# Two unused tiles in SBUF that shift what lies behind them, and the last first product one step earlier

## The chip, the cores and the metric

One core of a Trainium2 chip runs the kernel. The time is that of the device, in microseconds, for one launch; the kernel before was run three times. Beside these stands one profiled execution, of which the trace tells the start and duration of each instruction. In the views TensorE is PE (its weight loads PEld), VectorE is DVE, ScalarE is ACT, GpSimd is POOL, SyncE is SP.

## The reference

What is computed is a gated linear attention over 4 x 8 heads, 768 positions and head size 40, and behind it two feed-forward layers on 3072 tokens with 320 features and 2048 hidden units, all in float32:

```python
h = x @ w_in
g = np.maximum(h, 0.0) ** 2                                          # layer 0
g = np.where(h > 0.0, h, np.exp(np.minimum(h, 0.0)) - 1.0)           # layer 1
x = g @ w_out
```

The attention's output, heads side by side, is x of layer 0; the output of layer 0 is x of layer 1.

## The kernel before

**Tiles and steps.** The tokens are cut into 6 tiles of 512 (`NTILE`, `TT`), the hidden units into 16 blocks of 128 (`NF`). One step `k` is one layer, one token tile and one block of hidden units: 2 x 6 x 16 = 192 steps, 0 to 191, layer 0 first. Each float32 operand of a product is held as two fp32r parts, a high and a low one, and a product is the sum high x high + high x low + low x high.

- `mm1(k)`, the first product (L496): eight matmuls of 512 columns. A block of `w` is the stationary side, the tile's `xh` or `xl` the moving side; the sum is the PSUM tile `h`.
- `elem(k)` and `elem_lo(k)`, the elementwise part, into `ghi` and `glo`. In layer 0 ScalarE does most of it. In layer 1 ScalarE makes r, th and ex of h (L514, L515, L516), VectorE joins them (L517, L518, which reads h too), GpSimd rounds r into ghi (L519), and VectorE subtracts ghi from r into glo (L524).
- `mm2(k)`, the second product (L540). In layer 0 it is eight matmuls with `w` as the stationary and ghi or glo as the moving side, 512 columns. In layer 1 it is twelve, three for each of four accumulators, with ghi or glo as the stationary side and 320 columns of `w` as the moving one: ghi with the high weights, ghi with the low ones, glo with the high ones.
- `put(k)` at the last block of a tile copies the accumulators out and stores them.

**What sets the order.** The first 20 steps and much of the attention follow the table `ORDER`. From then on a loop over k writes the instructions: the first products up to step k + 2, their elementwise part, other work that is due, and then the second product of step k. So TensorE runs two first products ahead. On TensorE the order of the code is kept. In layer 1's last tile the other engines' instructions are placed by a scheduler when the kernel is built.

**Buffers.** Tiles are laid one behind the other in each SBUF partition, in the order of the pools: `const`, `w`, `raw`, `cvt`, `cvu`, `x`, `g`, `y`, and then the attention's. The `g` pool has two buffers each of `r`, `ghi` and `glo`, so those of step k are used again by step k + 2. The attention's pools are closed at layer 0's last tile, and the pools `by`, `bt`, `pa` and `pb` of layer 1 take their place. `h` has two buffers in `ph` and, from there on, two in `pb` for odd k.

Other matmuls that the prediction compares with: fillers without use (L659, bf16, 512 columns of ones, `dr`) and the three matmuls that make a mask early on (L613 to L615). L614's moving side `nst` is a row of 512 fp32r elements; L615's is `heads`, a view in which each value is repeated 128 times with step 0.

Of the kernel before, what the change touches and what calls it, by code (L numbers as in the profile page):

```python
# [6 lines left out]
F32 = mybir.dt.float32  # L7
F32R = mybir.dt.float32r
# [24 lines left out]
TT = 4 * L  # L33
# [30 lines left out]
def body(tc, qk, qp, kvo, gates, wq, ident_in, qkm_in, out):  # L64
# [4 lines left out]
    def pool(name, bufs=1, stack=es, **kw):  # L69
        return stack.enter_context(tc.tile_pool(name=name, bufs=bufs, **kw))  # L70
# [3 lines left out]
    negm_dr = dram.tile([NCH, B * H, L], F32, name="negm_dr")  # L74

    constp = pool("const")
    wp = pool("w", bufs=NF)
    rawp = pool("raw", bufs=3)
    cvt = pool("cvt", bufs=3)
    cvu = pool("cvu", bufs=2)  # L80
    xp = pool("x", bufs=2)
    gp = pool("g", bufs=2)
    yp = pool("y", bufs=3)
# [332 lines left out]
    def attn_pre(t):  # L416
        u, k = divmod(t, 4)
        if k == 0:
            units(u, lambda u: emit_E(2 * u))
            units(u - 1, norm)  # L420
            units(u + 1, kvo_load)
        elif k == 1:
            units(u, lambda u: emit_E(2 * u + 1), o_tanh, wk_mult)
            if u + 1 == NPLAIN // 2:
                qk_load(NPLAIN + 1)
        elif k == 2:
            units(u + 1, lambda v: qk_hi(2 * v), lambda v: qk_hi(2 * v + 1), lambda v: mask(2 * v))
            units(u + 1, lambda v: mask(2 * v + 1), lambda v: qk_stack(2 * v), lambda v: qk_stack(2 * v + 1))
        else:
            units(u + 2, lambda v: mb_load(2 * v), lambda v: mb_load(2 * v + 1), qp_load)  # L430
            units(u + 2, lambda v: qk_load(2 * v), lambda v: None if v == NPLAIN // 2 else qk_load(2 * v + 1))
        if k % 2 == 0:
            gate_at(t + 12, gate_store)
            if t == 10:
                gate_put(1)
            gate_at(t + 18, gate_load)

    def attn_pe(t):
        u, k = divmod(t, 4)
        if k == 0:  # L440
            units(u, lambda u: [f() for f in scores(2 * u)])
        elif k == 1:
            units(u - 1, lambda w: [f() for f in trans(w)])
            units(u, lambda u: [f() for f in scores(2 * u + 1)])
        for c in range(1, NCH):
            if t == (16 * c - 9 if c > 1 else 9):
                for f in gate_cols(c):
                    f()

    def attn_mul(t):  # L450
        u, k = divmod(t, 4)
        if k < 2:
            units(u, lambda u: emit_P(2 * u + k))
        if k == 1:
            units(u - 1, x_hi)
        if t % 16 == 7 and 0 < t // 16 < NCH - 1:
            gate_put(t // 16 + 1)

    def attn_post(t):
        u, k = divmod(t, 4)  # L460
        if k == 1:
            units(u - 1, x_lo)
        if k % 2:
            gate_at(t + 15, gate)
        else:
            gate_at(t + 14, gate_exp)
# [6 lines left out]
    def turn(t):  # L473
        for f in (attn_pre, attn_pe, attn_mul, attn_post, attn_last):
            f(t)

    G, HB, ACC = {}, {}, {}
    steps = [(l, j, m, (0, TT)) for l in range(2) for j in range(NTILE) for m in range(NF)]
    bp = {}

    def mm1(k):
        l, j, m, (c0, c1) = steps[k]
        n = c1 - c0
        w = W[l, m]
        xh, xl = X[l * NTILE + j]
        ilo = WC + (0 if l else 64)
        h = (bp["h"] if "h" in bp and k % 2 else ph).tile([128, TT], F32, tag="h", name="h")
        seq = []
        for kk in range(2):
            ws = slice(kk * 128, kk * 128 + 128)  # L490
            wlo = slice(ilo + kk * 128, ilo + kk * 128 + 128)
            seq += [(w[:, ws], xh[:, kk, c0:c1]), (w[:, ws], xl[:, kk, c0:c1]), (w[:, wlo], xh[:, kk, c0:c1])]
        seq += [(w[:, 256:384], xh[:, 2, c0:c1]), (w[:, ilo + 256:ilo + 384], xh[:, 2, c0:c1])]
        HB[k] = h
        return [
            lambda i=i, a=a, b_=b_: pe.matmul(h[:, 0:n], lhsT=a, rhs=b_, start=(i == 0), stop=(i == len(seq) - 1))  # L496
            for i, (a, b_) in enumerate(seq)
        ]

    def elem(k):  # L500
        l, j, _, (c0, c1) = steps[k]
        n = c1 - c0
        h = HB.pop(k)[:, 0:n]
        r = gp.tile([128, TT], F32, tag="r", name="r")[:, 0:n]
        hi = gp.tile([128, TT], F32R, tag="ghi", name="ghi")[:, 0:n]
        lo = gp.tile([128, TT], F32R, tag="glo", name="glo")[:, 0:n]
        if l == 0:
            act.activation(out=r, in_=h, func=AF.Relu)  # L508
            act.activation(out=hi, in_=r, func=AF.Square)  # L509
            act.activation(out=r, in_=r, func=AF.Square)  # L510
        else:
            th = bp["t"].tile([128, TT], F32, tag="th", name="th")
            ex = bp["t"].tile([128, TT], F32, tag="ex", name="ex")
            act.activation(out=r, in_=h, func=AF.Relu, scale=-1.0)  # L514
            act.activation(out=th, in_=r, func=AF.Tanh, scale=0.5)  # L515
            act.activation(out=ex, in_=r, func=AF.Exp, scale=-1.0)  # L516
            dve.scalar_tensor_tensor(out=ex, in0=ex, scalar=1.0, in1=th, op0=ALU.add, op1=ALU.mult)  # L517
            dve.scalar_tensor_tensor(out=r, in0=h, scalar=0.0, in1=ex, op0=ALU.max, op1=ALU.subtract)  # L518
            pool_.tensor_scalar(out=hi, in0=r, scalar1=1.0, scalar2=1.0, op0=ALU.mult, op1=ALU.mult)  # L519
        G[k] = (hi, lo, r)  # L520

    def elem_lo(k):
        hi, lo, r = G[k]
        dve.tensor_tensor(out=lo, in0=r, in1=hi.bitcast(F32), op=ALU.subtract)  # L524
# [213 lines left out]
    def first(k):  # L738
        nonlocal nm
        todo = []  # L740
        while nm <= min(k, len(steps) - 1):
            for f in mm1(nm):
                f()
            todo.append(nm)
            nm += 1
        return todo

    for k in range(NK, len(steps)):
        l, j, m, _ = steps[k]
        if k == (NTILE - 1) * NF:  # L750
            early.close()
            es.enter_context(tc.manual_schedule(engines={pe.engine}))
            for e in (act, dve, pool_, sp):
                es.enter_context(tc.issue_after(next(i for i in reversed(nc.cur_bb.bb.instructions) if i.engine == e.engine)))
        last = l == 0 and j == NTILE - 1
        ts = []
        if l == 0 and j + 1 < NTILE:
            to = 16 * j + m + 22
            ts = list(range(nt, min(TEND, to)))
            nt += len(ts)  # L760
        if last and m == 0:
            ea.close()
            bp["y"] = pool("by", reuse_waits="tile")
            bp["t"] = pool("bt", bufs=2, reuse_waits="tile")
            bp["a"] = pool("pa", space=PSUM, reuse_waits="tile")
            bp["h"] = pool("pb", bufs=2, space=PSUM, reuse_waits="tile")
        for t in ts[:-1]:
            turn(t)
        for t in ts[-1:]:
            attn_pre(t)  # L770
        todo = first(k + 2)
        for t in ts[-1:]:
            attn_pe(t)
        for e in todo:
            elem(e)
        for t in ts[-1:]:
            attn_mul(t)
        for e in todo:
            elem_lo(e)
        for t in ts[-1:]:  # L780
            attn_post(t)
        if l == 0 and j == 1 and 3 < m < 7:
            w_next(0, w_load)
        if l == 0 and 1 < j < NTILE - 1:
            if m == 5:
                w_next(1, w_top, w_low)
            if m == 8:
                w_next(2, w_add)
                w_next(0, w_load)
        if last or l == 1 and j == 0 and m % 2 == 0:  # L790
            if w_n[3] < min(w_n[2], NF + m if last else 2 * NF):
                w_next(3, w_hi, w_lo)
            if w_n[1] < min(w_n[0], NF + m if last else 2 * NF):
                w_next(1, w_top, w_low)
                w_next(2, w_add)
            if w_n[0] < min(w_n[2] + 3, 2 * NF):
                w_next(0, w_load)
        jn = j + 1 if l else 0
        if (l or last) and jn < NTILE:
            if m == 1:  # L800
                y_load(jn)
            if m in (4, 6, 8, 10):
                y_split(jn, (m - 4) // 2)
        for f in mm2(k):
            f()
        put(k)
        for t in ts[-1:]:
            attn_last(t)
# [63 lines left out]
```

## Time and profile before

| | |
|---|---|
| median of 3 runs | 824.15 us |
| lowest, highest | 822.54, 828.32 us |
| profiled execution, its time | 824.49 us |
| profiled execution, its span | 822.7 us |
| TensorE busy | 813.8 us, 99% of the span |
| VectorE, ScalarE, GpSimd busy | 534.6, 521.3, 118.3 us |

The span runs from the first to the last instruction; 1.8 us of the execution lie around it. Matmuls overlap in the array, and their ends are modelled: what one costs is the distance from its start to the next one's start, not its own duration. A row "xN" in the timeline is N instructions in a row, with the start of the first and the end of the last.

### The profile page before, as it was taken

What the parts mean: (1) busy time and instruction counts of PE and PEld (TensorE: products, weight loads), DVE (VectorE), ACT (ScalarE), POOL (GpSimd) and SP (SyncE); (2) the same over time, 40 slices, a digit from 0 to 9 for tenths busy, and PEclk for the clock granted to TensorE, in tenths of its full rate; (3) what the DMA queues carried; (4) which work ended last, traced back from release to release, by engine and by line L of the source; (5) the groups of instructions that cost most, each with busy time, mean ns of one, the idle gap of its engine ahead of it and who ended that gap; (6) DMA issues with size and microseconds to landing.
All of it is one profiled execution on the core that took longest, in us unless ns stands there. A gap on an engine that the chain in (4) does not pass through costs nothing.

```text
span 822.7 us, 14139 instructions
## 1 busy us (share of the span) xinstructions
PE 813.8 (99%) x5289; PEld 683.6 (83%) x5289; DVE 534.6 (65%) x969; ACT 521.3 (63%) x972; POOL 118.3 (14%) x197
## 2 busy tenths in 40 slices
PE   9999999999999999999999999999999999999997
PEld 5677787888888888888878888988988988988986
DVE  6999878567666656564277765655655656655554
ACT  5789577677667776776588844644644645544543
POOL 4321113111111120000000011111111111111111
PEclk9999999999999999999999999999999999999999
DMA  8977258635454644431166310200200200000000
GB/s 255 309 274 223 67 149 232 198 112 151 114 172 130 184 131 160 150 112 38 50 195 199 100 39 0 84 2 1 84 1 1 85 1 0 33 1 2 33 1 32
DMA packets 47450, 84.31 MB, mean 102 GB/s; under 512 B 4023, under 2 KB 28311, under 8 KB 47383
## 3 DMA queue, kind: packets, MB, share of 16 engines
q1 hardware_dynamic: 47095, 83.10, 32.8%
q8 instruction: 41, 0.67, 0.4%
q10 hardware_dynamic: 288, 0.33, 0.1%
q14 instruction: 26, 0.21, 0.1%
HBM read 74.68 MB, written 8.73 MB: 101 GB/s over the span
## 4 chain that ended last, share of the span: by engine, by line
PE 89%; DMA 4%; DVE 3%; issue 2%; ACT 1%; POOL 1%; SPq 1%; POOLq 0%; DVEq 0%
PE h L496 41%; PE acc L540 39%; PE pv L326 2%; PE in L326 2%; PE s L315 1%; DMA kvo<-kvo 1%; DMA rqk<-qk 1%; PE in L384 1%; DMA mb<-negm_dr 1%; PE pv L331 1%; DMA raw<-wq 1%; ACT mb L296 0%; PE s L305 0%; DMA yr<-y_dr 0%; DVE glo L524 0%
## 5 line engine op out<-in xcount | busy, mean ns | idle before, releaser
L496 PE MATMUL h<-xh,w 128*128 128x512 f32 x1152 | 364.3, 398 | 0.0
L496 PEld LDWEIGHTS h<-xh,w 128*128 128x128 f32 x1152 | 216.1, 188 | 48.7 <-DVE w L147 0.2
L524 DVE TENSOR_TENSOR glo<-r,ghi 128x512 fp32r<-128x512 f32 x192 | 135.7, 709 | 166.9 <-ACT r L510 91.8
L540 PE MATMUL acc<-w,ghi 128*128 128x320 f32 x768 | 170.8, 308 | 0.6 <-POOL ghi L519 0.6
L514 ACT ACTIVATE r<-h 128x512 f32<-128x512 f32 x96 | 57.4, 597 | 161.6 <-PE h L496 160.0
L496 PE MATMUL h<-xl,w 128*128 128x512 f32 x384 | 151.7, 395 | 0.0
L540 PEld LDWEIGHTS acc<-w,ghi 128*128 128x128 f32 x768 | 132.2, 188 | 9.5 <-POOL ghi L519 0.9
L540 PE MATMUL acc<-ghi,w 128*128 128x512 f32 x480 | 130.3, 401 | 0.0
L540 PE MATMUL acc<-w,glo 128*128 128x320 f32 x384 | 118.3, 308 | 0.8 <-DVE glo L524 0.8
L519 POOL TENSOR_SCALAR ghi<-r 128x512 fp32r<-128x512 f32 x96 | 59.3, 618 | 360.6 <-DVE r L518 344.2
L540 PEld LDWEIGHTS acc<-ghi,w 128*128 128x128 f32 x480 | 88.3, 189 | 19.4 <-ACT y L567 0.3
L517 DVE SCALAR_TENSOR_TENSOR ex<-ex,th 128x512 f32<-128x512 f32 x96 | 66.5, 693 | 55.9 <-ACT ex L516 55.4
L509 ACT ACTIVATE ghi<-r 128x512 fp32r<-128x512 f32 x96 | 60.6, 631 | 50.8 <-PE acc L540 49.6
L508 ACT ACTIVATE r<-h 128x512 f32<-128x512 f32 x96 | 56.5, 589 | 47.1 <-PE h L496 45.1
L540 PE MATMUL acc<-glo,w 128*128 128x512 f32 x288 | 83.4, 397 | 0.0
L496 PEld LDWEIGHTS h<-xl,w 128*128 128x128 f32 x384 | 72.1, 188 | 12.3 <-DVE xl L401 0.2
L540 PEld LDWEIGHTS acc<-w,glo 128*128 128x128 f32 x384 | 72.0, 188 | 1.4 <-DVE glo L524 1.4
L518 DVE SCALAR_TENSOR_TENSOR r<-h,ex 128x512 f32<-128x512 f32 x96 | 66.3, 690 | 3.0
L540 PEld LDWEIGHTS acc<-glo,w 128*128 128x128 f32 x288 | 53.5, 188 | 12.9 <-DVE glo L524 0.2
L510 ACT ACTIVATE r<-r 128x512 f32<-128x512 f32 x96 | 60.8, 633 | 3.0
L515 ACT ACTIVATE th<-r 128x512 f32<-128x512 f32 x96 | 60.8, 634 | 2.8
L516 ACT ACTIVATE ex<-r 128x512 f32<-128x512 f32 x96 | 59.1, 615 | 0.0
(113 smaller groups left out, 786.0 us busy)
## 6 DMA issues: line engine op xcount, KB each, us to landing
raw<-wq SPq DMA_DIRECT2D x32, 704.0 KB, 4.2
rqk<-qk SPq DMA_DIRECT2D x32, 480.0 KB, 6.8
kvo<-kvo SPq DMA_DIRECT2D x24, 488.0 KB, 3.9
mb<-negm_dr SPq DMA_DIRECT2D x40, 256.0 KB, 6.9
y_dr<-y SPq DMA_DIRECT2D x18, 256.0 KB, 2.9
qp<-qp SPq DMA_DIRECT2D x16, 256.0 KB, 5.2
out<-y SPq DMA_DIRECT2D x22, 160.0 KB, 1.9
yr<-y_dr SPq DMA_DIRECT2D x12, 256.0 KB, 3.0
```

What stands on the lines that cost most here:

```text
L496: lambda i=i, a=a, b_=b_: pe.matmul(h[:, 0:n], lhsT=a, rhs=b_, start=(i == 0), stop=(i == len(seq) - 1))
L508: act.activation(out=r, in_=h, func=AF.Relu)
L509: act.activation(out=hi, in_=r, func=AF.Square)
L510: act.activation(out=r, in_=r, func=AF.Square)
L514: act.activation(out=r, in_=h, func=AF.Relu, scale=-1.0)
L515: act.activation(out=th, in_=r, func=AF.Tanh, scale=0.5)
L516: act.activation(out=ex, in_=r, func=AF.Exp, scale=-1.0)
L517: dve.scalar_tensor_tensor(out=ex, in0=ex, scalar=1.0, in1=th, op0=ALU.add, op1=ALU.mult)
L518: dve.scalar_tensor_tensor(out=r, in0=h, scalar=0.0, in1=ex, op0=ALU.max, op1=ALU.subtract)
L519: pool_.tensor_scalar(out=hi, in0=r, scalar1=1.0, scalar2=1.0, op0=ALU.mult, op1=ALU.mult)
L524: dve.tensor_tensor(out=lo, in0=r, in1=hi.bitcast(F32), op=ALU.subtract)
L540: ops.append(lambda: pe.matmul(o, lhsT=l_, rhs=r_, start=first and st, stop=last and sp_))
```

## The change

A tile `room` of 128 bytes is added ahead of the others in `const`, and one of 320 bytes at the end of `cvu`; nothing reads or writes either. The tiles behind them move. Of the built programs, the place in the partition as a remainder of 512 bytes:

| tile | before | after |
|---|---|---|
| `w`, and its high weights | 384 | 0 |
| low weights of layer 1's second product | 128 | 256 |
| `xh`, `xl`, `r`, `ghi`, `glo`, `dr`, `y`, `th`, `ex` | 64 | 0 |
| `raw` (three buffers) | 384, 448, 0 | 0, 64, 128 |
| attention: `rqk`, `qks` | 0 | 448 |
| attention: `mb`, `qp` | 256 | 192 |
| attention: `kvo` (two buffers) | 128, 448 | 64, 384 |

All but a few small tiles lie at multiples of 64 bytes in both.

The loop asks for first products up to step k + 3 in the last four steps, so at k = 188 both first(190) and first(191) are written. The elementwise part of step 191 takes `r`, `ghi` and `glo` from a pool `bg` of its own.

```diff
@@ -74,10 +74,13 @@
     negm_dr = dram.tile([NCH, B * H, L], F32, name="negm_dr")
 
     constp = pool("const")
+
+    constp.tile([128, 32], F32, name="room")
     wp = pool("w", bufs=NF)
     rawp = pool("raw", bufs=3)
     cvt = pool("cvt", bufs=3)
     cvu = pool("cvu", bufs=2)
+    cvu.tile([128, 80], F32, tag="room", name="room", bufs=1)
     xp = pool("x", bufs=2)
     gp = pool("g", bufs=2)
     yp = pool("y", bufs=3)
@@ -501,9 +504,10 @@
         l, j, _, (c0, c1) = steps[k]
         n = c1 - c0
         h = HB.pop(k)[:, 0:n]
-        r = gp.tile([128, TT], F32, tag="r", name="r")[:, 0:n]
-        hi = gp.tile([128, TT], F32R, tag="ghi", name="ghi")[:, 0:n]
-        lo = gp.tile([128, TT], F32R, tag="glo", name="glo")[:, 0:n]
+        g = bp["g"] if k == len(steps) - 1 else gp
+        r = g.tile([128, TT], F32, tag="r", name="r")[:, 0:n]
+        hi = g.tile([128, TT], F32R, tag="ghi", name="ghi")[:, 0:n]
+        lo = g.tile([128, TT], F32R, tag="glo", name="glo")[:, 0:n]
         if l == 0:
             act.activation(out=r, in_=h, func=AF.Relu)
             act.activation(out=hi, in_=r, func=AF.Square)
@@ -762,13 +766,14 @@
             ea.close()
             bp["y"] = pool("by", reuse_waits="tile")
             bp["t"] = pool("bt", bufs=2, reuse_waits="tile")
+            bp["g"] = pool("bg", reuse_waits="tile")
             bp["a"] = pool("pa", space=PSUM, reuse_waits="tile")
             bp["h"] = pool("pb", bufs=2, space=PSUM, reuse_waits="tile")
         for t in ts[:-1]:
             turn(t)
         for t in ts[-1:]:
             attn_pre(t)
-        todo = first(k + 2)
+        todo = first(k + 2 if k < len(steps) - 4 else k + 3)
         for t in ts[-1:]:
             attn_pe(t)
         for e in todo:
```

TensorE near the end, before: the last first product (h_8650, step 191) stands behind the second product of step 188.

```order
L496 MATMUL h_8617<-xh_7821,w_5427 128x512 x3
L540 MATMUL acc0_8238<-w_5344,ghi_8561 128x320 x2
L540 MATMUL acc0_8238<-w_5344,glo_8562 128x320
L540 MATMUL acc1_8239<-w_5344,ghi_8561 128x320 x2
L540 MATMUL acc1_8239<-w_5344,glo_8562 128x320
L540 MATMUL acc2_8240<-w_5344,ghi_8561 128x320 x2
L540 MATMUL acc2_8240<-w_5344,glo_8562 128x320
L540 MATMUL acc3_8241<-w_5344,ghi_8561 128x320 x2
L540 MATMUL acc3_8241<-w_5344,glo_8562 128x320
L496 MATMUL h_8650<-xh_7821,w_5512 128x512
L496 MATMUL h_8650<-xl_7822,w_5512 128x512
```

The same place after; h_8622 is step 190's, h_8631 step 191's.

```order
L499 MATMUL h_8622<-xl_7827,w_5432 128x512
L499 MATMUL h_8622<-xh_7826,w_5432 128x512 x3
L499 MATMUL h_8631<-xh_7826,w_5517 128x512
L499 MATMUL h_8631<-xl_7827,w_5517 128x512
L499 MATMUL h_8631<-xh_7826,w_5517 128x512 x2
L499 MATMUL h_8631<-xl_7827,w_5517 128x512
L499 MATMUL h_8631<-xh_7826,w_5517 128x512 x3
L544 MATMUL acc0_8243<-w_5349,ghi_8566 128x320 x2
L544 MATMUL acc0_8243<-w_5349,glo_8567 128x320
```

The first product of step 191 has moved ahead of the second product of step 188; the second products of 188 to 191 then follow each other.

VectorE's last elementwise rows, before, steps 190 and 191:

```order
L517 SCALAR_TENSOR_TENSOR ex_8630<-ex_8630,th_8629 128x512
L518 SCALAR_TENSOR_TENSOR r_8626<-h_8617,ex_8630 128x512
L524 TENSOR_TENSOR glo_8628<-r_8626,ghi_8627 128x512
L517 SCALAR_TENSOR_TENSOR ex_8663<-ex_8663,th_8662 128x512
L518 SCALAR_TENSOR_TENSOR r_8659<-h_8650,ex_8663 128x512
L524 TENSOR_TENSOR glo_8661<-r_8659,ghi_8660 128x512
```

And after, where ex_8655 belongs to step 191 and glo_8642 to step 190:

```order
L521 SCALAR_TENSOR_TENSOR ex_8644<-ex_8644,th_8643 128x512
L522 SCALAR_TENSOR_TENSOR r_8640<-h_8622,ex_8644 128x512
L521 SCALAR_TENSOR_TENSOR ex_8655<-ex_8655,th_8654 128x512
L528 TENSOR_TENSOR glo_8642<-r_8640,ghi_8641 128x512
L522 SCALAR_TENSOR_TENSOR r_8651<-h_8631,ex_8655 128x512
L528 TENSOR_TENSOR glo_8653<-r_8651,ghi_8652 128x512
```

L517 of step 191 (now L521) stands ahead of step 190's glo (now L528). On the other engines, and elsewhere on these two, the instructions stand in the same order in both programs.

## Rows read from the trace of the kernel before

**Rows 1.** The page, part 1: busy us (share of the span) xinstructions, by engine.

```profile
PE 813.8 (99%) x5289; PEld 683.6 (83%) x5289; DVE 534.6 (65%) x969; ACT 521.3 (63%) x972; POOL 118.3 (14%) x197
```

**Rows 2.** Windows: length, then busy us (instructions) by engine, clock, DMA share, GB/s.

```profile
500.00:800.00 300.00, 300.00 (x1656) 269.67 (x1655) 179.67 (x264) 157.63 (x281) 51.28 (x83) 1.00 0.07 22
```

**Rows 3.** Waits of TensorE from 812 us on: us in total, times, longest.

```profile
PE acc L540 <- POOL ghi L519: 0.6, 1, 0.6
```

**Rows 4.** Groups by line and shape: count, busy us, mean ns, idle before.

```profile
L496 PE MATMUL h<-xh,w 128*128 128x512 f32 x1152 | 364.3, 398 | 0.0
...
L540 PE MATMUL acc<-w,ghi 128*128 128x320 f32 x768 | 170.8, 308 | 0.6 <-POOL ghi L519 0.6
L496 PE MATMUL h<-xl,w 128*128 128x512 f32 x384 | 151.7, 395 | 0.0
...
L540 PE MATMUL acc<-ghi,w 128*128 128x512 f32 x480 | 130.3, 401 | 0.0
L540 PE MATMUL acc<-w,glo 128*128 128x320 f32 x384 | 118.3, 308 | 0.8 <-DVE glo L524 0.8
...
L540 PE MATMUL acc<-glo,w 128*128 128x512 f32 x288 | 83.4, 397 | 0.0
```

**Rows 5.** Timeline of TensorE in layer 0, near 401 us.

```profile
400.95 0.39 PE L496 MATMUL h<-xh,w 128*128 128x512 f32 x1
...
402.82 1.33 PE L540 MATMUL acc<-ghi,w 128*128 128x512 f32 x5
```

**Rows 6.** Timeline of all engines over the last 15 us.

```profile
808.78 0.46 PE L540 MATMUL acc<-w,ghi 128*128 128x320 f32 x2
...
809.07 0.31 PE L540 MATMUL acc<-w,glo 128*128 128x320 f32 x1
...
809.22 0.45 PE L540 MATMUL acc<-w,ghi 128*128 128x320 f32 x2
...
810.54 0.40 PE L496 MATMUL h<-xh,w 128*128 128x512 f32 x1
...
810.78 0.39 PE L496 MATMUL h<-xl,w 128*128 128x512 f32 x1
...
812.41 0.46 PE L540 MATMUL acc<-w,ghi 128*128 128x320 f32 x2
...
812.61 0.60 ACT L514 ACTIVATE r<-h 128x512 f32<-128x512 f32 x1 [1.85 <-PE h L496]
...
814.42 0.69 DVE L517 SCALAR_TENSOR_TENSOR ex<-ex,th 128x512 f32<-128x512 f32 x1 [0.69 <-ACT ex L516]
...
815.15 0.69 DVE L518 SCALAR_TENSOR_TENSOR r<-h,ex 128x512 f32<-128x512 f32 x1
...
815.79 0.30 PE L540 MATMUL acc<-w,glo 128*128 128x320 f32 x1
816.03 0.62 POOL L519 TENSOR_SCALAR ghi<-r 128x512 fp32r<-128x512 f32 x1 [3.02 <-DVE r L518]
816.67 0.69 DVE L524 TENSOR_TENSOR glo<-r,ghi 128x512 fp32r<-128x512 f32 x1 [0.83 <-POOL ghi L519]
...
816.70 0.56 PE L540 MATMUL acc<-w,ghi 128*128 128x320 f32 x2 [0.61 <-POOL ghi L519]
...
817.42 0.42 PE L540 MATMUL acc<-w,glo 128*128 128x320 f32 x1 [0.16 <-DVE glo L524]
...
818.85 0.30 PE L540 MATMUL acc<-w,glo 128*128 128x320 f32 x1
```

**Rows 7.** Timeline of TensorE near 16 us: start us, us, instruction.

```profile
16.24 0.40 PE L614 MATMUL h<-nst,selq 128*128 128x512 f32 x1
16.47 0.38 PE L615 MATMUL h<-sel,ast 128*128 128x512 f32 x1
16.69 1.04 PE L659 MATMUL dps<-dr 128*128 128x512 bf16 x4
```

**Rows 8.** Timeline of TensorE near 31 us.

```profile
31.00 2.12 PE L659 MATMUL dps<-dr 128*128 128x512 bf16 x9
```

## The prediction

> **What bounds the kernel now.** I read the page first [rows 1]. TensorE is busy for 813.8 of 822.7 us, 99%, and the next engine for 65%: the kernel ends when TensorE has got through its list. So only two things can shorten it: fewer nanoseconds for one matmul, or less waiting of TensorE. The windows say how little waiting there is [rows 2]: between 500 and 800 us TensorE is busy for all 300.00 us at clock 1.00 (the 2.4 GHz level), while VectorE works 180, ScalarE 158 and GpSimd 51 of them. The view of waits, asked for the end alone, finds TensorE held once, for 0.6 us, by the POOL instruction that makes ghi [rows 3].
>
> Next I took the price of one matmul, and that must come from starts, since the ends are modelled. The groups give the counts [rows 4]: 1152 + 384 first products and 480 + 288 second products of layer 0 stream 512 columns, which is 2304; 768 + 384 of layer 1 stream 320 columns, which is 1152. In layer 0 a chain of eight first products begins at 400.95 and what follows begins at 402.82 [rows 5]; in layer 1 the eight run from 810.54 to 812.41 [rows 6]. Both are 1.87 us: **233.75 ns for 512 columns**. Twelve products of 320 columns run from 808.78 to 810.54 [rows 6]: **146.7 ns**. Together 2304 x 233.75 + 1152 x 146.7 = 538.6 + 169.0 = 707.6 us, 86% of the span.
>
> Is there something to win in these? The trace has two kinds of 512-column matmul that are faster. The bf16 fillers: nine take 2.12 us, four take 1.04, so five more cost 1.08, 216 ns each [rows 7, 8]. And the product whose moving operand is `heads`, one value repeated along the row with step 0: it begins at 16.47 and the next at 16.69, 0.22 us, while its fp32r neighbour with an ordinary row took 0.23, from 16.24 to 16.47 [rows 7]. So about 17.75 ns of the 233.75 go with reading 512 consecutive 4-byte elements. The question of this change is whether the place of the row in its partition has a share in them.
>
> **The rooms.** They add no instruction. They move the const tiles and all from `w` to `cvu` by 128 bytes and what lies behind by 448, so that w, x, r, ghi, glo lie at remainder 0 of 512 in place of 384 and 64. Because no trace of a contiguous fp32r row of that length at remainder 0 exists here, I bound the effect.
>
> Upper end of the gain: the whole excess goes. 17.75 x 2304 = 40.9 us; for 320 columns the same share, 10.7 ns as worked out below, x 1152 = 12.3 us; in all 53.2 us (a third of the layer-1 products read low weights that come to lie at remainder 256; without them 49.1). Lower end: a loss is not excluded. Between neighbours of such a chain the timeline shows steps of 0.23 and 0.24 us (810.54 to 810.78 is one of the longer, [rows 6]); were all 0.24, +2.7% of 707.6, 18.9 us.
>
> Which end is near? Layer 1 tests the place already. Its high weights stream from remainder 384 of 512, its low weights from remainder 128, and ghi and glo are the stationary side there at 64. Of the three products for one acc, the second reads the low weights and the others the high; the two with ghi take 0.29 us, from 808.78 to 809.07, and the one with glo 0.15, to 809.22 [rows 6]: high and low cost alike. A row of 1280 bytes from 384 crosses three multiples of 512, one from 128 crosses two: a price for each crossing would make the one dearer by half than the other. The excess also goes with the columns, not with the matmul: 17.75 ns in 512 and in 320, where a row without the excess would take 320/2.4 = 133.3 ns and the 2.7 that the filler's 216 has over 512/2.4, 146.7 - 136.0 = 10.7 ns; the ratio is 1.66 where the columns have 1.6. A start off a boundary would cost once a matmul. The excess behaves as a rate at which 4-byte rows are read, and a rate has no boundary. I therefore take **0 us**, and keep both ends.
>
> The Trainium skill (TensorE: Matmul & The Clock Gate, "Back-to-back issue gap") gives N/2.4 + 2.5 ns between matmuls at the full clock whatever the type, 216 ns for 512 columns; the bf16 fillers agree and the fp32r products, 18 ns longer, do not. By it 2304 x 17.9 = 41 us of layer 0 and the first products should be there to take. Against that, the Trainium skill (SBUF — State Buffer, "Specifications (TRN2)") puts the cost of a read at each crossing into a new 16-byte line. Every place of before is a multiple of 64 bytes and crosses as many such lines as one at 512, so by this rule the rooms change nothing; no run here shows the line itself.
>
> What the rooms push out of place: rqk and qks go from remainder 0 to 448, mb and qp from 256 to 192, kvo by 448. They serve the attention products and their DMAs. Those run under the list of TensorE; the attention's rows are short, and its places of before were already mixed. I price this at 0, within 1 us either way.
>
> **The last first product a step early.** This lies wholly in the last 12 us and I can place it by the clock of before [rows 6]. Call the last two steps 190 and 191. Before, TensorE runs second(188) 808.78 to 810.54, first(191) to 812.41, second(189), second(190), whose last matmul starts at 815.79 and would be followed at 815.94. But ghi(191) is there only at 816.65: first(191) ends 812.41, ScalarE starts 0.20 later, VectorE's L517 another 1.81 later, L518 0.73 after that, POOL 0.88 after that, and glo follows at 816.67. So second(191) starts at 816.70, 0.76 late, and its first glo product at 817.42 in place of 816.99, 0.43 late: **1.19 us** of waiting, more than the view of waits counts since the modelled ends of matmuls cover a part.
>
> After, first(191) runs 808.78 to 810.65 and second(188), (189), (190) follow without a break to 815.93. The order shows VectorE's new row: L517(191) now stands ahead of glo(190). On ScalarE, L514(190) starts at 808.98 and its three take 1.81, so L514(191) can start at 810.85 as its h is ready; L517(191) at 812.66; glo(190), queued behind it, needs ghi(190), ready at 813.01 (before: 816.65 less the 3.63 of a step), and runs 813.38 to 814.07, well before second(190)'s first glo product at 814.46. L518(191) 814.10, POOL 814.98, ghi(191) ready 815.60, glo(191) 815.62 to 816.31. Second(191) can start at 815.93 without waiting for ghi; its first glo product would be due at 816.22 and waits to about 816.37: 0.15 us. The gain is 1.19 - 0.15 = **1.04 us**. The copies and stores at the end hang on the last matmul (818.85), so all of it reaches the end. The h tile of first(191) is that of step 187, whose L518 ended three steps before; the r, ghi, glo of its own spare a wait on second(189). If glo(190) came 0.4 us late, the gain would shrink by what is over. No DMA moves; SP's list is the same.
>
> **Sum.** The profiled execution took 824.49 us, 1.8 more than its span and 0.34 above the median of the three timed runs, 824.15. 824.49 - 0 - 1.04 = 823.45 for such an execution; against the median, **823.1 us**. That is 0.13%, and the three runs of before lie between 822.54 and 828.32: a change under 1% is not told from none.
>
> **Rivals.** (1) The place was the whole excess. For it: the excess is real and specific to read rows [rows 5, 7]; no long row of before stands at 0 or 256 of 512. Against: it goes by columns, and 384 and 128 cost alike. 824.15 - 53.2 - 1.04 = 769.9 us. The rule of the Trainium skill on the gap (TensorE: Matmul & The Clock Gate, "Back-to-back issue gap") would come out near this time. (2) The place has a small share: the chains would step by 0.230 us, the shorter of the two values of the timeline (16.24 to 16.47, [rows 7]), in place of 0.23375, 1.6% of 707.6 us = 11.3 us: 811.8 us. (3) It ends slower: stationary and moving rows are read at the same time, and before their remainders differ (384 and 64); after, both are 0, and if equal places get into each other's way every product pays. At the 0.24 of the longest steps this is +18.9: 842 us; from 2.7 ns a matmul (8.2 + 1.04 us over 3456 products) it is more than 1%. Against: weights at 384 and at 128 against x at 64 gave the same 1.87. (4) The early product does nothing, because glo(190) is late behind L517(191) by as much as is won: 824.1 us.
>
> **How the numbers follow.** Forecast 0.70 (its own range 821 to 828, the spread of the runs), rival 4 0.05, rival 1 0.09, rival 2 0.09, rival 3 0.07. The range from 811 to 829 holds the forecast, rivals 2 and 4, 0.84; it leaves out 1 and 3. Faster by over 1% are rivals 1 and 2, 0.18; slower is rival 3, 0.07; 0.75 remains.
>
> **What would show it.** Right: chains of eight still 1.87 us and of twelve 1.76 in the timeline of both layers; L540 at the end with no wait on ghi and 0.1 to 0.2 us on glo; last matmul some 1 us nearer to the end of second(190). Wrong: chains of eight at 1.73 (rival 1), 1.84 (rival 2) or 1.90 and more (rival 3), which would be seen in every step between 500 and 800 us; or a gap ahead of second(190)'s glo product (rival 4).

## The result, and the profile after

The changed kernel takes 814.33 us (median of 4 runs, 811.65 to 817.27); the kernel before, run again beside it, 826.06 us (4 runs, 822.54 to 828.32). The ratio on record is 0.9872, 95% interval [0.9833, 0.991]: 1.3% faster (the two medians divided would give 0.986; here and below the recorded ratio is used). The time lies in the range on record, but near the end that a rival held, not where the forecast stood. The profiled execution took 815.76 us with a span of 814.0 (before 824.49 and 822.7).

The page after, part 1, as in [rows 1]:

```profile
PE 801.6 (98%) x5285; PEld 683.0 (84%) x5289; DVE 535.6 (66%) x969; ACT 520.2 (64%) x972; POOL 118.4 (15%) x197
```

TensorE is the bound as before and is busy for 12.2 us less; the other engines work as long as they did. The chain of waits of the changed kernel (the work that ended last, followed back from the end), near 400 us (layer 0) and near 690 us (layer 1); the columns are start us, us, what:

```profile
400.65 1.81 PE acc L544 x8
402.47 1.81 PE h L499 x8
...
691.75 1.84 PE h L499 x8
693.59 1.75 PE acc L544 x12
695.34 1.84 PE h L499 x8
```

L499 is the first product (L496 before), L544 the second (L540). A chain of eight products of 512 columns takes 1.81 us in layer 0, 226 ns each, and 1.84 in layer 1, where it was 1.87 in both [rows 5, 6]. Twelve of 320 columns take 1.75, where it was 1.76: they gain next to nothing.

The 1.84 is not spread evenly over its eight products. The timeline of TensorE in the changed kernel, one chain of layer 1:

```profile
691.59 0.39 PE L499 MATMUL h<-xh,w 128*128 128x512 f32 x1
...
692.74 0.84 PE L499 MATMUL h<-xh,w 128*128 128x512 f32 x3
693.42 0.45 PE L544 MATMUL acc<-w,ghi 128*128 128x320 f32 x2
```

The first five take 1.15 us, 230 ns each, and the last three 0.68, 227 each. Layer 0 is alike where other matmuls stand between the chains. Taken from the starts between 94 and 440 us, a 512-column product that comes first behind another matmul costs 306.4 ns before and 305.0 after on average, the second to seventh 233.1 and 230.2, and those from the eighth on 233.5 and 227.2. So the full gain is there only some products into a row of them.

How much of the 8.7 us of span that is, the first products tell. Timeline of TensorE in the changed kernel, first product of layer 0 and of layer 1:

```profile
35.93 0.58 PE L499 MATMUL h<-xh,w 128*128 128x512 f32 x1
...
457.08 0.39 PE L499 MATMUL h<-xh,w 128*128 128x512 f32 x1
```

And in the kernel before:

```profile
35.06 0.58 PE L496 MATMUL h<-xh,w 128*128 128x512 f32 x1
...
464.55 0.39 PE L496 MATMUL h<-xh,w 128*128 128x512 f32 x1
```

From first product to first product, layer 0 takes 421.15 us in place of 429.49, 8.3 less. In layer 1 a step, one chain of eight and one of twelve, takes 3.59 in place of 3.63, 3.8 us over its 96 steps. The end gives 1.0, as follows below. That is 13.1. Given back are 0.87 us ahead of the first product (35.93 for 35.06) and 2 us at the start of layer 1, where TensorE waits. The view of waits of the changed kernel from 440 us on:

```profile
PE acc L544 <- DVE glo L528: 2.6, 1, 2.6
```

Its timeline shows what stands ahead of that glo on VectorE (yr is the tile that layer 1's input is loaded into):

```profile
466.92 0.69 DVE L604 TENSOR_TENSOR yr<-yr 128x512 f32<-128x512 f32 x1 [1.67 <-DMA yr<-y_dr]
...
468.57 0.68 DVE L528 TENSOR_TENSOR glo<-r,ghi 128x512 fp32r<-128x512 f32 x1
...
469.31 0.63 PE L544 MATMUL acc<-w,glo 128*128 128x320 f32 x1 [2.64 <-DVE glo L528]
```

VectorE's first work on layer 1's second tile (L604) waits for its load, and glo waits in the queue behind it. Before, TensorE waited 0.66 us at this place:

```profile
475.00 0.42 PE L540 MATMUL acc<-w,glo 128*128 128x320 f32 x1 [0.66 <-DVE glo L524]
```

The same instruction of VectorE waited 1.48 us for its load there, so the load alone does not make the difference. Both profiled executions also have one stretch at half the clock; the windows of the changed kernel and of the one before (length, busy us of PE, PEld, DVE, ACT, POOL, clock, DMA, GB/s) place them:

```profile
469.00:473.00 4.00, 3.69 (x13) 3.55 (x14) 3.50 (x6) 1.75 (x3) 0.62 (x1) 0.57 0.00 0
```

```profile
88.00:92.00 4.00, 4.00 (x26) 2.93 (x27) 2.73 (x6) 1.28 (x3) 0.00 (x0) 0.58 0.00 0
```

At 0.57 and 0.58 of four us, 2.4 GHz for a part and 1.2 for the rest, it costs some 1.7 us in each. In the kernel before it lies in layer 0, so 1.7 of the 8.3 us there come from it, and it stands against layer 1 after. 13.1 - 0.87 - 2.0 - 1.7 = 8.5 us, of 8.7 measured. The run with the early product alone, reported below, checks the first of these: its operands have the places of before, no such stretch falls into its layer 0, and that takes 462.83 - 35.02 = 427.81 us. Against it the changed kernel gains 6.7 us, and 8.3 - 1.7 is 6.6.

The stretch of the changed kernel begins where the wait for glo ends; from 465 to 469 us the granted clock is still 1.00. The two other runs that wait about as long there have one behind it too: granted clock 0.58 from 467 to 471 us with the second buffer (wait 2.51 us) and 0.57 from 475 to 479 with the rooms alone (2.34). So these 1.7 us may belong to the wait; that was not tested.

The end, in the timeline of the changed kernel (the last two steps are 190 and 191, as in the prediction):

```profile
803.04 0.45 PE L544 MATMUL acc<-w,ghi 128*128 128x320 f32 x2
...
804.96 0.62 POOL L523 TENSOR_SCALAR ghi<-r 128x512 fp32r<-128x512 f32 x1 [3.09 <-PE acc L544]
805.05 1.06 DVE L521 SCALAR_TENSOR_TENSOR ex<-ex,th 128x512 f32<-128x512 f32 x1 [0.40 <-ACT ex L520]
...
806.03 0.68 DVE L528 TENSOR_TENSOR glo<-r,ghi 128x512 fp32r<-128x512 f32 x1
...
806.55 0.46 PE L544 MATMUL acc<-w,ghi 128*128 128x320 f32 x2
...
806.85 0.33 PE L544 MATMUL acc<-w,glo 128*128 128x320 f32 x1
...
807.40 0.62 POOL L523 TENSOR_SCALAR ghi<-r 128x512 fp32r<-128x512 f32 x1 [1.83 <-DVE r L522]
...
808.05 0.69 DVE L528 TENSOR_TENSOR glo<-r,ghi 128x512 fp32r<-128x512 f32 x1 [0.74 <-POOL ghi L523]
...
808.33 0.46 PE L544 MATMUL acc<-w,ghi 128*128 128x320 f32 x2
...
808.80 0.41 PE L544 MATMUL acc<-w,glo 128*128 128x320 f32 x1
...
810.22 0.31 PE L544 MATMUL acc<-w,glo 128*128 128x320 f32 x1
```

The four second products run from 803.04 to the last matmul at 810.22, 7.18 us. Before, they took 818.85 - 808.78 less the 1.87 of the first product among them, 8.20 [rows 6]. The early product gives 1.02 us. There is no wait for ghi; the first glo product of step 191 begins 0.47 after the pair ahead of it, where 0.29 is usual: 0.18 us of waiting are left.

### The profile page after: what moved, and what is told of

Same layout as the page of the kernel before. It is cut to its first block, busy times and chain, and to the rows that moved or that the text cites. A ratio compares the mean times of both kernels' runs of the same rounds, so it can differ in the third digit from the quotient of the medians.

```text
span 814.0 us, 14133 instructions
## 1 busy us (share of the span) xinstructions
PE 801.6 (98%) x5285; PEld 683.0 (84%) x5289; DVE 535.6 (66%) x969; ACT 520.2 (64%) x972; POOL 118.4 (15%) x197
## 4 chain that ended last, share of the span: by engine, by line
PE 80%; DVE 7%; DMA 4%; ACT 3%; issue 3%; SPq 1%; POOL 1%; DVEq 0%; POOLq 0%; ACTq 0%
PE h L499 36%; PE acc L544 36%; PE pv L329 2%; DMA rqk<-qk 2%; DVE ct L140 2%; PE in L329 2%; DMA yr<-y_dr 1%; PE s L318 1%; DVE glo L528 1%; DVE w L150 1%; PE in L387 1%; ACT ct L135 1%; DMA mb<-negm_dr 1%; PE pv L334 1%; ACT cu L130 1%
## 5 line engine op out<-in xcount | busy, mean ns | idle before, releaser
L499 PE MATMUL h<-xh,w 128*128 128x512 f32 x1152 | 358.5, 393 | 0.0
L499 PEld LDWEIGHTS h<-xh,w 128*128 128x128 f32 x1152 | 216.4, 188 | 44.7 <-DVE w L150 0.6
L528 DVE TENSOR_TENSOR glo<-r,ghi 128x512 fp32r<-128x512 f32 x192 | 136.8, 714 | 162.1 <-ACT r L514 87.8
L544 PE MATMUL acc<-w,ghi 128*128 128x320 f32 x768 | 170.9, 310 | 0.0
L499 PE MATMUL h<-xl,w 128*128 128x512 f32 x384 | 150.7, 393 | 0.0
L544 PEld LDWEIGHTS acc<-w,ghi 128*128 128x128 f32 x768 | 133.0, 189 | 7.4 <-POOL ghi L523 0.2
L544 PE MATMUL acc<-ghi,w 128*128 128x512 f32 x480 | 127.2, 394 | 0.0
L544 PE MATMUL acc<-w,glo 128*128 128x320 f32 x384 | 119.6, 311 | 2.7 <-DVE glo L528 2.6
L544 PEld LDWEIGHTS acc<-ghi,w 128*128 128x128 f32 x480 | 87.8, 188 | 17.4 <-ACT y L571 0.3
L521 DVE SCALAR_TENSOR_TENSOR ex<-ex,th 128x512 f32<-128x512 f32 x96 | 67.0, 698 | 53.3 <-ACT ex L520 52.8
L544 PE MATMUL acc<-glo,w 128*128 128x512 f32 x288 | 81.7, 392 | 0.0
L499 PEld LDWEIGHTS h<-xl,w 128*128 128x128 f32 x384 | 72.3, 188 | 11.0 <-DVE xl L404 0.2
L544 PEld LDWEIGHTS acc<-w,glo 128*128 128x128 f32 x384 | 72.6, 189 | 3.2 <-DVE glo L528 3.2
L544 PEld LDWEIGHTS acc<-glo,w 128*128 128x128 f32 x288 | 53.4, 188 | 11.5 <-DVE glo L528 0.4
```

The source lines that it names most:

```text
L544: ops.append(lambda: pe.matmul(o, lhsT=l_, rhs=r_, start=first and st, stop=last and sp_))
```

## The experiments

All of them state their edit against the kernel before unless said otherwise; where only rooms are told, the order at the end is that of before (k + 2, no pool `bg`). "Stationary" is the block of `w` in first products and layer 0's second products, "moving" the row of x, ghi or glo; places are remainders of 512 bytes. Lines of an edit that only follow from those shown are left out. The kernel before, run beside them, had medians of 823.35 us (the first four experiments), 823.98 (the next four) and 823.12 (the last four).

**The early product alone.**

```diff
+        g = bp["g"] if k == len(steps) - 1 else gp
...
+            bp["g"] = pool("bg", reuse_waits="tile")
...
-        todo = first(k + 2)
+        todo = first(k + 2 if k < len(steps) - 4 else k + 3)
```

> Only the early last first product with its own buffers; no rooms, so w stays at 384 and x, r, ghi, glo at 64 of 512. Theory P (the place of the rows makes the gain, the early product about 1 us): chains of eight stay at 1.87 us, the time falls by 1.0 us, to about 0.999 of before. Rival T (the early product makes most of the gain): 0.99 of before with chains unchanged.

822.99 us beside 823.35, ratio 0.9992 [0.9971, 1.0013], and chains of eight at 1.87 in the chain of waits:

```profile
399.40 1.87 PE h L497 x8
401.27 1.87 PE acc L542 x8
```

A gain of 1.02 us would be 0.9988, inside an interval that also holds none. So the early product isn't where the 1.3% are.

**The rooms alone.**

```diff
+    constp.tile([128, 32], F32, name="room")
...
+    cvu.tile([128, 80], F32, tag="room", name="room", bufs=1)
```

> Only the two rooms, k + 2 to the end. Theory P: chains of eight at 1.81 to 1.83 us, the time 0.988 to 0.99 of before, the last second product still 1.2 us late. Rival T: 0.999 of before, chains at 1.87.

815.18 us, ratio 0.9901 [0.987, 0.9932], chains of eight at 1.81:

```profile
399.99 1.81 PE h L499 x8
401.80 1.81 PE acc L544 x8
```

The last second product is late again as in the kernel before, in the view of waits:

```profile
PE acc L544 <- POOL ghi L523: 0.6, 1, 0.6
```

The rooms make the gain.

**Which operand's place: x alone, then w alone.** For x at 0 with w at 384:

```diff
+    cvu.tile([128, 112], F32, tag="room", name="room", bufs=1)
```

> One room of 448 bytes behind cvu: x, r, ghi, glo at 0 of 512, w still at 384; k + 2 to the end. Theory M (the place of the moving row decides; in these chains it is x, ghi or glo in layer 0 and x in layer 1): chains of eight at 1.81 to 1.83, the time as with both rooms, 0.99. Rival S (the place of the stationary block decides): 1.87 and no change of time. Rival B (both must be at 0): between, or 1.87.

822.63 us, ratio 0.9981 [0.9955, 1.0007]; the chains:

```profile
399.07 1.86 PE h L498 x8
400.93 1.86 PE acc L543 x8
```

For w at 0 with x at 64:

```diff
+    constp.tile([128, 32], F32, name="room")
...
+    cvu.tile([128, 96], F32, tag="room", name="room", bufs=1)
```

> Room of 128 bytes ahead of const and one of 384 behind cvu: w at 0 of 512, x, r, ghi, glo at 64 as before; k + 2 to the end. Theory M: chains of eight at 1.87, no change of time. Rival S: 1.81 to 1.83 and 0.99. Rival B: 1.87.

817.04 us, ratio 0.9921 [0.9898, 0.9944]; the chains:

```profile
399.53 1.83 PE acc L544 x8
401.37 1.83 PE h L499 x8
```

Moving rows at 0 alone bring almost nothing, so theory M, that they decide, falls. Stationary blocks at 0 alone bring about two thirds of the fall in a chain, 1.87 to 1.83 of 1.87 to 1.81. I then took the stationary side for the cause, and asked which places suit it.

**Places of w, with x at 0.** At 256:

```diff
+    constp.tile([128, 96], F32, name="room")
...
+    cvu.tile([128, 16], F32, tag="room", name="room", bufs=1)
```

> Rooms sized so that w lies at 256 of 512 and x, r, ghi, glo at 0; k + 2 to the end. The stationary block of a first product is 128 x 4 = 512 bytes in a partition. Theory Q (a block should start at a multiple of 256): chains of eight in layer 0 at 1.81 to 1.83 us, time as with both rooms, 815. Rival F (it should start at a multiple of 512, so as not to reach over one): 1.85 to 1.87, 822; only layer 1's low weights, which then lie at 0, would be short.

814.54 us, ratio 0.9894 [0.9858, 0.993]: as good as both at 0. A block of 512 bytes at 256 reaches over a multiple of 512, and that costs nothing; rival F falls.

```profile
398.54 1.81 PE h L499 x8
400.36 1.81 PE acc L544 x8
```

At 128:

```diff
+    constp.tile([128, 64], F32, name="room")
...
+    cvu.tile([128, 48], F32, tag="room", name="room", bufs=1)
```

> w at 128 of 512, x, r, ghi, glo at 0; k + 2 to the end. Theories Q and F: chains of eight at 1.85 to 1.87, time 822. Rival U (384 alone is bad, or any multiple of 128 other than 384 is good): 1.81 to 1.83, 815.

822.38 us, ratio 0.9981 [0.9964, 0.9998]:

```profile
400.32 1.86 PE h L499 x8
402.17 1.86 PE acc L544 x8
```

At 64:

```diff
+    constp.tile([128, 48], F32, name="room")
...
+    cvu.tile([128, 64], F32, tag="room", name="room", bufs=1)
```

> w at 64 of 512, x, r, ghi, glo at 0; k + 2 to the end. Theories Q and F: chains of eight at 1.85 to 1.87 or more, 822 or later; rows at 64 were no worse than at 128 as moving rows, so the same as w at 128 is expected.

824.95 us, ratio 1.0014 [0.9993, 1.0035]:

```profile
399.31 1.86 PE h L499 x8
401.17 1.87 PE acc L544 x8
```

Both as theory Q had it: a stationary block wants a multiple of 256.

**w at 0, x at 128.**

```diff
+    constp.tile([128, 32], F32, name="room")
...
+    cvu.tile([128, 112], F32, tag="room", name="room", bufs=1)
```

> w at 0 of 512, x, r, ghi, glo at 128; k + 2 to the end. With x at 64 the 512-column step was between both rooms and before (chain of eight 1.82 to 1.83 in place of 1.81, 817 us). If the moving row counts by multiples of 128: 1.81, 815 us; if by 256 or 512: 1.82 to 1.83, 817 us.

822.27 us, ratio 0.9955 [0.992, 0.999], and chains that are as long as with w at 128 and x at 0:

```profile
400.31 1.86 PE h L499 x8
402.17 1.86 PE acc L544 x8
```

Neither expectation was met, and theory Q falls with it: the stationary block stands at 0, and the chain is slow. Put by the distance, stationary less moving as a remainder of 256, all kernels so far fall in line: 0 is 1.81, 64 (the kernel before and w at 64) 1.87, 128 (three kernels) 1.86, 192 (w at 0, x at 64) 1.83.

**The test of the distance: both at 128.**

```diff
+    constp.tile([128, 64], F32, name="room")
...
+    cvu.tile([128, 80], F32, tag="room", name="room", bufs=1)
```

> w, x, r, ghi, glo all at 128 of 512; k + 2 to the end. So far the 512-column step went by the distance between the stationary block and the moving row, as a remainder of 256: 0 fast, 64, 128 and 192 slower. Theory D (the distance decides): a step of sixteen products in layer 0 at 3.62 to 3.64 us, as with both at 0, time 815. Rival A (both must start at a multiple of 256): 3.71 to 3.73, time 822.

814.47 us, ratio 0.9878 [0.9835, 0.9921]; the chains:

```profile
398.54 1.81 PE acc L544 x8
400.35 1.81 PE h L499 x8
```

Two operands that are slow at 128 one by one are fast at 128 together. Theory D holds and rival A falls. This closes a square of four kernels, w and x each at 0 or 128: 1.81 on one diagonal, 1.86 on the other. It also rules out the tiles that move along. The kernel with w at 128 and x at 0 has all that lies ahead of the second room where both at 128 has it, and all behind it where both at 0 has it; the one with w at 0 and x at 128 has it the other way round. Both are slow with places that are fast in another kernel.

**Distances of 32.** x at 32, w at 0:

```diff
+    constp.tile([128, 32], F32, name="room")
...
+    cvu.tile([128, 88], F32, tag="room", name="room", bufs=1)
```

> w at 0 of 512, x, r, ghi, glo at 32: stationary less moving is 224 of 256, between 192 (3.66 us a step of layer 0) and 0 (3.63). Theory D: 3.62 to 3.67, time 814 to 818. Rival G (only multiples of 64 are read well): 3.72 or more, 822 or later.

823.99 us, ratio 1.0004 [0.9987, 1.0022]:

```profile
398.74 1.87 PE acc L544 x8
400.60 1.87 PE h L499 x8
```

And w at 32, x at 0:

```diff
+    constp.tile([128, 40], F32, name="room")
...
+    cvu.tile([128, 72], F32, tag="room", name="room", bufs=1)
```

> w at 32 of 512, x, r, ghi, glo at 0: stationary less moving is 32, between 0 (3.63 us a step of layer 0) and 64 (3.73). Theory D: 3.63 to 3.73, time 815 to 823, slower than the mirror image with x at 32. Rival G: 3.72 or more for both.

823.96 us, ratio 1.0006 [0.9987, 1.0025]:

```profile
399.57 1.87 PE h L499 x8
401.43 1.87 PE acc L544 x8
```

Both are as slow as before. My guess of a smooth curve between the points was wrong for 224, and the mirror images are alike; rival G, that places off a multiple of 64 are read worse, fits these two but was not tried with a distance of 0. For 32 and 224 the distance is therefore not shown to be the cause.

**A second buffer for the wait at layer 1's start**, against the changed kernel:

```diff
-            bp["y"] = pool("by", reuse_waits="tile")
+            bp["y"] = pool("by", bufs=2, reuse_waits="tile")
```

> The changed kernel with a second buffer for yr, so that the load of layer 1's second tile needn't wait for the last read of the first. In the changed kernel VectorE waits 1.67 us for that load near 465 us, and TensorE behind it 2.64 us for glo. If that load is the cause, TensorE's wait falls to 1 us or less and the time by 1.5 to 2 us. Rival: VectorE is simply behind there (weights of layer 1 to be split), and the wait stays over 2 us, the time unchanged.

813.75 us (5 runs, 812.74 to 815.36), ratio 0.987 [0.9845, 0.9895], which cannot be told from the changed kernel's 0.9872 [0.9833, 0.991]. TensorE still waits 2.51 us. The timeline shows why nothing came of it:

```profile
465.66 0.69 DVE L604 TENSOR_TENSOR yr<-yr 128x512 f32<-128x512 f32 x1 [1.53 <-DMA yr<-y_dr]
...
468.05 0.63 PE L544 MATMUL acc<-w,glo 128*128 128x320 f32 x1 [2.51 <-DVE glo L528]
```

VectorE waits for the load as before (1.53 us for 1.67), and the view of SyncE's queue still has the issue of that load 11.2 us behind a VectorE instruction of the first tile (L607). So the second buffer did not bring the load forward, and the experiment does not tell whether an earlier load would. That wait was 0.66 us in the kernel before, 1.34 with the early product alone, 2.34 with the rooms alone and 1.35 with w at 256. It does not go with VectorE's wait for the load, 1.37 us with the rooms alone and 1.83 with w at 256; why it differs stays open.

The ten placements in one table (places as remainders of 512; distance is stationary less moving, as a remainder of 256; us of eight products from the chains above):

| stationary, moving | distance | eight products, layer 0 | median us |
|---|---|---|---|
| 0, 0 (rooms alone) | 0 | 1.81 | 815.18 |
| 256, 0 | 0 | 1.81 | 814.54 |
| 128, 128 | 0 | 1.81 | 814.47 |
| 0, 64 | 192 | 1.83 | 817.04 |
| 384, 0 | 128 | 1.86 | 822.63 |
| 128, 0 | 128 | 1.86 | 822.38 |
| 0, 128 | 128 | 1.86 | 822.27 |
| 64, 0 | 64 | 1.86 to 1.87 | 824.95 |
| 0, 32 and 32, 0 | 224, 32 | 1.87 | 823.99, 823.96 |

## Why the prediction was right, and where it was wrong

**What bounds the kernel: right.** TensorE's list sets the end, the gain came from the price of a matmul and from the end of the list, and the prices worked out from starts (233.75 and 146.7 ns) are those that the experiments without a gain show again.

**The rooms at 0 us: wrong, and this is the step that failed.** The text said "The excess behaves as a rate at which 4-byte rows are read, and a rate has no boundary." Two arguments carried it. The first was that places 384 and 128 cost alike. They did, but they had to: against x at 64, weights at 384 and at 128 are 64 apart as a remainder of 256, and layer 1's ghi at 64 is 192 from both places of its moving rows. The trace held different places at the same distance, and I read it as a test of the place. The second was that the excess over the filler's step goes by columns, 17.75 to 10.7 ns for 512 to 320. That was chance: at distance 0 the 512-column product takes 226.25 ns, 10 over the filler's 216, and the 320-column one 1.75 / 12 = 145.8, some 10 over 136.0. What stays is about the same for each matmul, and what goes, some 7 ns (7.5 by chains read to 0.01 us), belongs almost alone to the 512-column products. Why the 320-column ones hardly mind the distance stays open. The 230 ns of layer 1's first products come from the first five of each chain, behind the 320-column ones, as shown above; why these keep a longer step stays open too.

**The size.** 7.5 ns over the 1536 products of layer 0 would be 11.5 us. 8.3 - 1.7 = 6.6 came in, in part because the products next behind other matmuls gain 1 to 3 ns and not 7; the rest was not placed. Layer 1 gave 3.8: 2.9 from 3.75 ns over its 768 first products, the rest from the twelves. In all that is 10.4 us. Rival 2 ("The place has a small share") had 11.3. That this is near was luck: it took the shorter of two rounded steps for all 512-column products and the same share for the others, and the step fell below it in layer 0 and hardly at all at 320 columns. Rival 3 had the right parts, two reads whose places meet, with the wrong sign: equal places are the best ones, not the worst. That the two reads disturb each other is argued from the dependence on the distance; no view shows the collision itself, and no run separates a read of weights from a read of the moving row. The Trainium skill (TensorE: Matmul & The Clock Gate, "Step-by-step: what each phase is for") says that the two reads of TensorE have ports of their own, and that loading the next weights takes nothing from the running matmul. Here eight products with the same operands cost 1.81 or 1.86 us by the places of the two relative to each other. If the reads are the cause, the measurement does not agree; that they are was argued, not shown.

**The rule of 16-byte lines** (the Trainium skill, SBUF — State Buffer, "Specifications (TRN2)", as in the prediction) spoke for no effect, and the place had one; every place tried is a multiple of 32 bytes, so the lines crossed were as many in each kernel, and the rule cannot be what decided here.

**What was pushed out of place, priced at 0 within 1 us: held.** The first product starts 0.87 us later; the view of waits of the whole run has 1.0 us for a load of rqk there. The run with the second buffer has the same places until layer 0's last tile and starts its first product sooner than the kernel before (35.06):

```profile
34.92 0.58 PE L499 MATMUL h<-xh,w 128*128 128x512 f32 x1
```

So the 0.87 us are not a price of the places.

**The early product: right, by its steps.** 1.04 us were worked out and 1.02 measured; 0.15 us of waiting for glo were left in the forecast and 0.18 in the trace; ghi held nothing up. One thing was missed: L521 of step 191 took 1.06 us in place of 0.69, beside the POOL instruction (804.96 to 805.58). The two other runs with the early product have the same, 1.07 and 1.06 us, and in all three the other fifteen of this instruction in the last tile, beside no work of POOL, take 0.69 each. The glo of step 190 queued behind it came 0.3 us later than worked out and was still done at 806.71, ahead of its use at 806.85.

**The range.** It held because its lower end was set by rival 2; the forecast's own 821 to 828 did not hold. That the time lies inside is therefore no sign that the forecast's mechanism for the rooms was right.

## What to carry to other kernels

Where matmuls follow each other without a gap and still take longer than the fastest of their shape in the trace, try to bring the stationary block and the moving row to the same remainder of 256 bytes with an unused tile: here 448 bytes in two tiles gave 1%. What counted was the same remainder, at 0 and at 128 alike; others were not tried. Expect the full gain in long rows of such matmuls only. Before taking different places in a trace for a test of the place, write down what else was equal in them, the distances above all. A move that aligns everything to one number can be right for another reason than the number.

## What the runs showed of the hardware that was not expected

- In layer 0, away from other matmuls, eight fp32r products of 512 columns with 128 x 128 stationary blocks take 1.81 us where stationary and moving rows start at the same remainder of 256 bytes (three placements), 1.83 at a distance of 192 (one), 1.86 at 128 (three) and 1.86 to 1.87 at 64, 32 and 224 (at the last two one operand is also off a multiple of 64). Twelve of 320 columns take 1.75 or 1.76 at all of them.
- The saving builds up. Behind a chain of 320 columns the first five 512-column products still take 230 ns each, the next three 227 (changed kernel, layer 1).
- A VectorE instruction of 0.69 us with both inputs in SBUF took 1.06 us beside a GpSimd instruction that was running over part of it (three runs).
